# Complex weights' length by sine and cosine of the arc tangent, third-order norm roots, and all stores on one queue, in an S4 and shift-MLP kernel

## The chip, the cores and the metric

One core of a Trainium2 chip. Its engines run instruction streams of their own: TensorE (PE) multiplies matrices, VectorE (DVE) and ScalarE (ACT) work elementwise, GpSimd (POOL) is all but unused here, and SyncE (SP) issues most of the DMA transfers. ACT can issue transfers too. ACT evaluates functions from a table set, and an instruction of its own, ACT_TABLE_LOAD, changes the set. Waits between engines go over semaphores. The metric is the device time of the whole program in microseconds (us); lower is better.

## The reference

```python
x  = A_u                                   # 1 x 2048 x 512
xn = layernorm(x)

# s: 512 channels with 128 complex states each
dt = exp(log_dt)
K  = einsum("dn,dnl,dn->dl", C, exp(dt*A*l), dt*B).real     # 512 x 2048
s  = irfft(rfft(xn, 4096) * rfft(K, 4096))[:2048] + xn * Dskip

# g: token mixing by shifts, then an MLP
h  = gelu(layernorm(xn) @ w1)              # quarters of h shifted by +1, -1, +2, -2 rows
x1 = xn + shifted(h) @ w2
g  = silu(x1 + gelu(layernorm(x1) @ w3) @ w4)    # w3: 512 x 1376

out = x + s * g
```

The complex weights B·C·dt of the first part are kept as magnitude and phase. For a product with parts wr and wi the kernel forms the ratio `rat` of the smaller to the larger absolute value; the magnitude is the larger one times sqrt(1 + rat²), and the phase comes from the arc tangent of `rat`.

## The kernel before

The program is recorded first and issued afterwards. Functions such as `params`, `token_mixing`, `tables`, `mlp`, `products`, `gate`, `inverse` and `finish` record every operation in a `Plan`, through one recorder for each engine (`V` DVE, `A` ACT, `T` PE, `Q` SP) and one, `E`, for work that two may do. `Plan.order` then schedules the list. The table `DUE` gives the priority of every operation, the string `PIN` says which of two engines takes an `E` operation, and models of instruction fetch (`FETCH`) and of PE's clock say when an operation could start. Where PE would wait, the scheduler fills the wait with dummy matmuls of the identity matrix. So almost every instruction has line 499 in the profile, dummies have 498 and table loads 496; the tiles' names tell the work apart.

The work stands in this order. `loads` brings in the input X and the parameters. `params(0)` and `params(1)` form magnitude (`am`) and phase (`ph`) of the weights, half of the channels each, in tiles of 128x256: `tm` holds the temporaries `ta` and `tb`, `sr` holds `side` and `rat`, and `pn` holds the results. `token_mixing` takes norms (`ln_first`, `ln_second`, both through `rstd` with its tile `rs`), multiplies by w1 and w2 and starts the transform of xn. `tables` builds the exponentials and sines from which the convolution's kernel comes. `mlp` runs for eight groups of two of the 16 row blocks, `GROUPS` = 1 to 7 and then 0, between stages of the convolution. For each group w4's products are collected in two accumulators (tile `pa`), one for each row block, and DVE then adds them to X. `gate` applies Silu, `inverse` makes the convolution's result (`zin` in, `pc` out) and multiplies it in, and `finish` adds `xr`, which is u once more, and stores four strips of 32 partitions. The last group is handled in two pieces, one for each row block, all others in one: 36 stores in all.

`rstd` starts from a guess by integer arithmetic on the bits and makes three Newton steps of three DVE instructions each, in eleven calls. A store of `finish` is an `E` operation, so `PIN` gives it to SP's queue or to ACT's; 22 are on SP and 14 on ACT. The transfers of both queues take completion semaphores in turn from one set of eight (`DMAHW0` to `DMAHW7`), and each transfer waits until the one before it on its semaphore has ended.

Of the kernel before, what the change touches and what calls it, by code (L numbers as in the profile page):

```python
# [13 lines left out]
AF = mybir.ActivationFunctionType  # L14
# [5 lines left out]
P = 128  # L20
# [11 lines left out]
INV_2PI = float(np.float32(1.0 / (2.0 * np.pi)))  # L32
QUARTER_PI = float(np.float32(np.pi / 4.0))
# [63 lines left out]
class Op:  # L97
# [20 lines left out]
SPAN, LEFT, LEAST = 0.224, 0.3, 0.8  # L118
# [7 lines left out]
FETCH = 1.5, 5.0, 2.5, 0.5  # L126
# [168 lines left out]
class Plan:  # L295
# [115 lines left out]
    def order(self):  # L411
# [20 lines left out]
        while len(out) < len(ops):  # L432
# [22 lines left out]
            if e == "PE":  # L455
# [3 lines left out]
                if pick.fresh and t - free[e] > LEAST:  # L459
                    start = max(free[e], pick.free_at)  # L460
                    pick.fill = max(0, int((t - start - LEFT) / SPAN))
                    if pick.fill:
                        words.wait(start, pick.fill * SPAN, 4 * pick.fill, chan)
                        t = max(t, clock.run(start, pick.fill * SPAN))
# [1115 lines left out]
```

## Time and profile before

| | us |
| --- | --- |
| median of 3 runs | 536.68 |
| the runs | 536.22 to 537.21 |
| the profiled execution | 537.38 |
| its span | 535.6 |
| ACT's table loads, 48 of 1283 ns | 61.6 |
| first store issued (from the span's start) | 511.5 |
| last store issued | 532.9 |

The span runs from the first to the last instruction that the profiler saw; the execution's time has 1.8 us more around it. In a row, "128x256 f32<-128x256 f32" gives partitions by elements out and in, "x8" the number of records, and the bracket how long the engine stood idle before it and what ended that. A matmul of 32-bit numbers leaves two records. In the rows by group the figures behind the bar are busy time, mean nanoseconds of one, and idle time before. In the rows by tile the three figures are shortest, median and longest in nanoseconds, then the first and the last start. A row of windows gives the window, its length, and the busy time of PE, PE's weight loads, DVE, ACT and POOL; PEclk is the granted clock of PE as a share of full speed. A row of waits gives the total, the number and the longest. Times of rows are from the span's start.

### The profile page before, as it was taken

What the parts mean: (1) busy time and instruction counts of PE and PEld (TensorE: products, weight loads), DVE (VectorE), ACT (ScalarE), POOL (GpSimd) and SP (SyncE); (2) the same over time, 40 slices, a digit from 0 to 9 for tenths busy, and PEclk for the clock granted to TensorE, in tenths of its full rate; (3) what the DMA queues carried; (4) which work ended last, traced back from release to release, by engine and by line L of the source; (5) the groups of instructions that cost most, each with busy time, mean ns of one, the idle gap of its engine ahead of it and who ended that gap; (6) DMA issues with size and microseconds to landing.
All of it is one profiled execution on the core that took longest, in us unless ns stands there. A gap on an engine that the chain in (4) does not pass through costs nothing.

```text
span 535.6 us, 14336 instructions
## 1 busy us (share of the span) xinstructions
PE 511.1 (95%) x6055; PEld 333.1 (62%) x6055; DVE 450.9 (84%) x783; ACT 400.8 (75%) x597; POOL 0.7 (0%) x6
## 2 busy tenths in 40 slices
PE   8789999999999999999999999999999999999992
PEld 8776666774343666565676676666655666566650
DVE  6899999999999999999999999999553267754593
ACT  4999999999998999998989999885336315322420
POOL 0000000000000000000000000000000000000000
PEclk9899999999999999999999999999999999999997
DMA  7994689983886506456333643547989859979986
GB/s 192 258 222 160 227 249 254 281 233 121 296 269 221 101 7 163 140 194 178 112 129 70 180 158 107 118 164 207 251 332 320 282 175 286 258 234 275 310 252 186
DMA packets 95329, 109.44 MB, mean 204 GB/s; under 512 B 40289, under 2 KB 74337, under 8 KB 94369
## 3 DMA queue, kind: packets, MB, share of 16 engines
q1 hardware_dynamic: 94592, 106.95, 69.4%
q10 hardware_dynamic: 672, 1.57, 1.0%
q8 instruction: 47, 0.77, 0.6%
q14 instruction: 18, 0.14, 0.1%
HBM read 64.46 MB, written 37.75 MB: 191 GB/s over the span
## 4 chain that ended last, share of the span: by engine, by line
PE 68%; DVE 10%; ACT 10%; DMA 7%; issue 2%; SPq 2%; ACTq 0%; DVEq 0%
PE pb L499 22%; PE pa L499 22%; PE pd L499 13%; PE pc L499 11%; DVE pt L499 7%; DMA X<-in_A_u_dram 4%; ACT pt L499 3%; SPq L499 2%; ACT ue L499 2%; DVE X L499 1%; ACT L496 1%; DMA scr_Ud<-ue 1%; ACT wst L499 1%; DMA cst<-c_gp 1%; DMA rawC<-in_A_B_re_dram 1%
## 5 line engine op out<-in xcount | busy, mean ns | idle before, releaser
L499 PE MATMUL pb<-x1T,w3h 128*128 128x256 f16 (+1 forms) x1056 | 124.9, 273 | 0.0
L499 PE MATMUL pa<-w4h,ghl 128*128 128x512 f16 (+1 forms) x528 | 123.4, 380 | 0.0
L499 PEld LDWEIGHTS <-w3h 128*128 128x128 f16 (+1 forms) x1056 | 102.6, 100 | 28.8 <-issue 11.6
L499 PEld LDWEIGHTS <-ghl 128*128 128x128 f16 (+1 forms) x528 | 49.4, 98 | 60.6 <-issue 9.2
L499 ACT ACTIVATE g<-pb,wsc 128x512 f32<-128x512 f32 (+1 forms) x48 | 30.7, 650 | 47.6 <-PE pb L499 43.6
L499 ACT ACTIVATE pt<-pt 128x2048 f32<-128x2048 int32 x32 | 61.0, 1908 | 2.4 <-DVE pt L499 2.3
L496 ACT ACT_TABLE_LOAD x48 | 61.6, 1283 | 1.6 <-PEq L1568 0.7
L499 DVE TENSOR_TENSOR pt<-mag,pt 128x1024 f32<-128x1024 f32 x48 | 58.1, 1215 | 0.1
L499 PE MATMUL pd<-w,hT 128*128 128x512 f32 x116 | 53.3, 600 | 2.4 <-DVE X L499 1.9
L499 DVE SCALAR_TENSOR_TENSOR ghl<-g,wsc,ghl 128x512 f16<-128x512 f32 (+1 forms) x48 | 33.5, 700 | 11.6 <-ACT ghl L499 11.3
L499 ACT ACTIVATE mag<-par 128x128 f32<-128x128 f32 x160 | 41.1, 463 | 0.1
L499 ACT ACTIVATE ghl<-g,wsc 128x512 f16<-128x512 f32 (+1 forms) x35 | 24.0, 688 | 20.5 <-PE pa L499 19.0
L499 PEld LDWEIGHTS pd<-w,hT 128*128 128x128 f32 x116 | 21.1, 190 | 27.7 <-issue 23.3
L499 DVE TENSOR_TENSOR pt<-pt 128x2048 f32<-128x2048 f32 x16 | 36.4, 2281 | 0.9 <-ACT pt L499 0.9
L499 PEld LDWEIGHTS pc<-pt 128*32 128x32 f32 x2048 | 29.5, 110 | 8.4 <-issue 5.8
L499 PE MATMUL pc<-pt 128*32 128x64 f32 x2048 | 32.4, 220 | 1.9 <-DVE pt L499 1.0
L499 ACT ACTIVATE pt<-pt,halfpi 128x2048 f32<-128x2048 f32 x16 | 32.0, 1999 | 0.1
L499 PE MATMUL pb<-xT,w 128*128 128x256 f32 x128 | 29.6, 383 | 1.4 <-ACT xT L499 1.4
L499 DVE TENSOR_TENSOR pr<-pd,uin 128x1024 f32<-128x1024 f32 x16 | 19.3, 1219 | 11.5 <-PE pd L499 11.5
L499 PEld LDWEIGHTS pb<-xT,w 128*128 128x128 f32 x128 | 23.6, 190 | 7.8 <-ACT xT L499 3.3
L499 DVE TENSOR_TENSOR pr<-pd,kh 128x1024 f32<-128x1024 f32 x16 | 19.3, 1218 | 6.7 <-PE pd L499 6.0
L499 PE MATMUL pb<-xT,w1h 128*128 128x256 f16 x192 | 22.5, 273 | 0.0
(160 smaller groups left out, 787.8 us busy)
## 6 DMA issues: line engine op xcount, KB each, us to landing
wst<-in_B_w_dram SPq DMA_DIRECT2D x20, 512.0 KB, 5.1
scr_Ud<-ue SPq DMA_DIRECT2D x16, 512.0 KB, 3.9
uin<-scr_Ud SPq DMA_DIRECT2D x32, 256.0 KB, 4.3
cst<-c_gp SPq DMA_DIRECT2D x16, 384.0 KB, 4.0
scr_Uh<-uh SPq DMA_DIRECT2D x8, 512.0 KB, 3.2
scr_Kfa<-k1e SPq DMA_DIRECT2D x8, 512.0 KB, 3.7
kin<-scr_Kfa SPq DMA_DIRECT2D x16, 256.0 KB, 4.1
scr_Zda<-z1e SPq DMA_DIRECT2D x8, 512.0 KB, 5.0
```

Source lines behind the costliest of these rows:

```text
L496: self.engines["ACT"].preload_act_table_set(SETS[table])
L499: ins = [getattr(self.engines[op.eng], name)(*args, **kw).ins for name, args, kw in op.calls]
```

## The change

Six things change.

1. `rstd` makes one step of third order (four instructions) and one Newton step (three) in place of three Newton steps (nine).
2. `params` takes the length as max·(cos φ + rat·sin φ), with φ the arc tangent of `rat`. Arctan and two Sin run together from one table set; Square, Sqrt and the set of Sqrt go. DVE has two instructions more for each half.
3. All stores go to SP's queue.
4. For the last group, each pair of w4's products is two planned operations, one for each accumulator, where it was one.
5. Constants of the scheduler's models differ: `FETCH`, and a factor `FILLED` on the number of dummies in a wait. There are 34 dummies where there were 57, beside 36 at the start that stay.
6. `DUE` and `PIN` hold other values throughout, so that most instructions stand at other places. The rows further down show three places.

```diff
+CUBIC = 0.375 ** 0.5, -1.25 / 0.375 ** 0.5, 1.875
...
-FETCH = 1.5, 5.0, 2.5, 0.5
+FETCH = 1.8, 5.0, 2.8, 0.7
...
-                    pick.fill = max(0, int((t - start - LEFT) / SPAN))
+                    pick.fill = max(0, int((t - start - LEFT) * FILLED / SPAN))
...
     def rstd(dst, var, x, t, by=1.0):
         V.tensor_scalar(x, var, EPS, None, op0=ALU.add)
         guess(dst, x)
-        for f in (1.0, 1.0, by):
-            V.scalar_tensor_tensor(t, dst, -0.5 * f, dst, op0=ALU.mult, op1=ALU.mult)
-            V.tensor_mul(t, t, x)
-            V.scalar_tensor_tensor(dst, t, 1.5 * f, dst, op0=ALU.add, op1=ALU.mult)
+        V.scalar_tensor_tensor(t, dst, CUBIC[0], dst, op0=ALU.mult, op1=ALU.mult)
+        V.tensor_mul(t, t, x)
+        V.scalar_tensor_tensor(t, t, CUBIC[1], t, op0=ALU.add, op1=ALU.mult)
+        V.scalar_tensor_tensor(dst, t, CUBIC[2], dst, op0=ALU.add, op1=ALU.mult)
+        V.scalar_tensor_tensor(t, dst, -0.5 * by, dst, op0=ALU.mult, op1=ALU.mult)
+        V.tensor_mul(t, t, x)
+        V.scalar_tensor_tensor(dst, t, 1.5 * by, dst, op0=ALU.add, op1=ALU.mult)
...
-        A.activation(ta, rat, AF.Square)
-        A.activation(tb, ta, AF.Sqrt, bias=1.0)
-        V.tensor_mul(am, am, tb)
+        with plan.together(table=TABLES[AF.Arctan]):
+            A.activation(ph, rat, AF.Arctan)
+            A.activation(ta, ph, AF.Sin)
+            A.activation(tb, ph, AF.Sin, bias=halfpi[:, 0:1], scale=-1.0)
+        V.tensor_mul(ta, ta, rat)
+        V.tensor_add(ta, ta, tb)
+        V.tensor_mul(am, am, ta)
         by_step(am, am, ld)
-        A.activation(ph, rat, AF.Arctan)
...
-            for r in range(4):
-                E.store(ov[ORDER[r]][:, x], X[32 * r : 32 * r + 32, x])
+            by_r(X[:, x, c], ov[:, :, :, x][..., c], True)
...
-                with plan.together(cost=DOWN):
-                    for i in range(2):
+                for some in ((0,), (1,)) if g == GROUPS[-1] else ((0, 1),):
+                    with plan.together(cost=DOWN * len(some) / 2):
+                        for i in some:
```

The first place is ACT in the first half of `params`. Before (`tm<-sr` is Square, `pn<-sr` the Arctan, the `tm<-tm` between the loads Sqrt; `EB` and `mag` are exponentials):

```order
L499 ACTIVATE tm<-sr 128x256 [waits DVE_49]
L496 ACT_TABLE_LOAD
L499 ACTIVATE pn<-sr 128x256
L496 ACT_TABLE_LOAD
L499 ACTIVATE tm<-tm 128x256 [waits Activation_49]
L499 ACTIVATE wst,ssq<-wst 128x1024 [waits DMAHW4_49]
L496 ACT_TABLE_LOAD
L499 ACTIVATE EB<-par 128x128 x12
```

The same place in the changed program, from the load before the Arctan on (`tm<-pn` and `tm<-pn,halfpi` are the sines):

```order
L496 ACT_TABLE_LOAD
L499 ACTIVATE pn<-sr 128x256 [waits DVE_49]
L499 ACTIVATE tm<-pn 128x256 [waits Activation_49]
L499 ACTIVATE tm<-pn,halfpi 128x256
L496 ACT_TABLE_LOAD
L499 ACTIVATE mag<-par 128x128 x8
L499 ACTIVATE EB<-par 128x128 x12
L499 ACTIVATE pn<-pn,ld 128x128 [waits DVE_49]
```

Three loads have become two, and the load of the weights' squares (`wst`) has moved behind the exponentials.

The second place is the end of PE's stream: the last w4 products (`pa`), of which `ghl_486` and `ghl_488` are the left sides and each has three for either accumulator, and the last inverse transforms (`pc`). Before:

```order
L499 LDWEIGHTS ghl_488 [waits DVE_49]
L499 MATMUL pa_97<-w4h_205,ghl_488 128x512
L499 LDWEIGHTS ghl_488
L499 MATMUL pa_97<-w4h_205,ghl_488 128x512
L499 MATMUL pc_98<-zin_556,is2_82 32x256 [waits DMAHW7_49,DVE_49]
L499 MATMUL pc_98<-zin_556,is2_82 32x256 x7
L499 MATMUL pc_98<-zin_557,is2_82 32x256 [waits DMAHW5_49]
L499 MATMUL pc_98<-zin_557,is2_82 32x256 x7
```

The end of PE's stream in the changed program:

```order
L499 LDWEIGHTS ghl_486
L499 MATMUL pa_97<-w4h_201,ghl_486 128x512
L499 LDWEIGHTS ghl_488
L499 MATMUL pa_97<-w4h_205,ghl_488 128x512 [waits DVE_49]
L499 LDWEIGHTS ghl_488
L499 MATMUL pa_97<-w4h_205,ghl_488 128x512
L499 LDWEIGHTS ghl_488
L499 MATMUL pa_97<-w4h_205,ghl_488 128x512
L499 MATMUL pc_98<-zin_557,is2_82 32x256 [waits DMAHW2_49]
L499 MATMUL pc_98<-zin_557,is2_82 32x256 x7
```

The products of the second accumulator now stand by themselves at the end, the last three with a wait for DVE, and the first set of inverse transforms (`zin_556`) stands ahead of this place.

The third place is the end of ACT's stream, with its stores and the last Silu (`X<-X` 128x512). Before:

```order
L499 DMA out_dram<-X 32x1024 [waits DMAHW2_49,DVE_49]
L499 DMA out_dram<-X 32x1024 [waits DMAHW4_49]
L499 ACTIVATE X<-X 128x512 [waits DVE_49] x2
L499 DMA out_dram<-X 32x1024 [waits DMAHW6_49]
L499 DMA out_dram<-X 32x512 [waits DMAHW0_49,DVE_49,Activation_49]
L499 DMA out_dram<-X 32x1024 [waits DMAHW2_49]
L499 DMA out_dram<-X 32x512 [waits DMAHW4_49,DVE_49,Activation_49]
L499 DMA out_dram<-X 32x512 [waits DMAHW5_49]
L499 DMA out_dram<-X 32x512 [waits DMAHW7_49]
```

In the changed program SP's stream ends with all of the last group's stores, and ACT's with the Silu:

```order
L499 DMA out_dram<-X 32x512 [waits DMAHW1_49,DVE_49,Activation_49]
L499 DMA out_dram<-X 32x512 [waits DMAHW2_49]
L499 DMA out_dram<-X 32x512 [waits DMAHW3_49]
L499 DMA out_dram<-X 32x512 [waits DMAHW4_49,DVE_49,Activation_49]
L499 DMA out_dram<-X 32x512 [waits DMAHW5_49]
L499 DMA out_dram<-X 32x512 [waits DMAHW6_49]
```

The 14 stores of ACT stand on SP, and their completion semaphores now follow one another in SP's own order.

More of the change, by code (lines that the diff above doesn't have):

```diff
@@ L117 @@
 WINDOW, LOW, HIGH, HALF = 3.4133, 0.64, 0.87, 0.6
-SPAN, LEFT, LEAST = 0.224, 0.3, 0.8
+SPAN, LEFT, LEAST, FILLED = 0.224, 0.3, 0.8, 0.87
 SCRATCH = 512
@@ L647 @@
     E = Either(plan)
-    xv = u[0].rearrange("(t r s) d -> r t s d", r=4, s=S)
-    ov = out[0].rearrange("(t r s) d -> r t s d", r=4, s=S)
+    xv = u[0].rearrange("(t b a s) d -> a b t s d", a=2, b=2, s=S)
+    ov = out[0].rearrange("(t b a s) d -> a b t s d", a=2, b=2, s=S)
     dram = ctx.enter_context(tc.tile_pool(name="dram", bufs=1, space=DRAM))
@@ L832, in loads @@
     def loads():
-        by_r(X[:, 0:2], xv[:, :, 0:2])
+        by_r(X[:, 0:2], xv[:, :, :, 0:2])
         load_w(w1, w1s, stile)
@@ L1192, in gate @@
     def gate(g):
-        for x, _ in pieces(g):
-            A.activation(X[:, x], X[:, x], AF.Silu)
+        for x, _, c in pieces(g):
+            A.activation(X[:, x, c], X[:, x, c], AF.Silu)
     def inverse(hf, g):
@@ L1209, in inverse @@
                 return
-            for x, k in pieces(g):
-                V.tensor_mul(X[:, x], X[:, x], pair[:, k])
+            for x, k, c in pieces(g):
+                V.tensor_mul(X[:, x, c], X[:, x, c], pair[:, k, c])
             return
@@ L1221, in finish @@
             xr[q] = at(xrs.pop(), [P, 4, D], F32, "xr")
-            by_r(xr[q], xv[:, :, 4 * q : 4 * q + 4])
-        for x, k in pieces(g):
-            V.tensor_add(X[:, x], X[:, x], xr[q][:, 2 * (g % 2) : 2 * (g % 2) + 2][:, k])
-            for r in range(4):
-                E.store(ov[ORDER[r]][:, x], X[32 * r : 32 * r + 32, x])
+            by_r(xr[q], xv[:, :, :, 4 * q : 4 * q + 4])
+        for x, k, c in pieces(g):
+            V.tensor_add(X[:, x, c], X[:, x, c], xr[q][:, 2 * (g % 2) : 2 * (g % 2) + 2][:, k, c])
+            by_r(X[:, x, c], ov[:, :, :, x][..., c], True)
     def pow2_scale(cols, dst_s, dst_inv, target):
@@ L1443, in pieces @@
         if g != GROUPS[-1]:
-            return [(slice(2 * g, 2 * g + 2), slice(0, 2))]
-        return [(2 * g + k, k) for k in range(2)]
+            return [(slice(2 * g, 2 * g + 2), slice(0, 2), slice(0, D))]
+        return [(2 * g + k, k, slice(0, D)) for k in range(2)]
     def mlp(g):
@@ L1476, in mlp @@
                 fn = FT[j][1]
-                with plan.together(cost=DOWN):
-                    for i in range(2):
-                        for lg, lw in ((0, 0), (0, 1), (1, 0)):
-                            T.matmul(
-                                accs[i], ghl[:fn, lg, a, i * P : (i + 1) * P], w4t[jp][:fn, a, lw],
-                                start=j == 0 and lg == 0 and lw == 0,
-                                stop=j == len(FT) - 1 and lg == 1,
-                            )
+                for some in ((0,), (1,)) if g == GROUPS[-1] else ((0, 1),):
+                    with plan.together(cost=DOWN * len(some) / 2):
+                        for i in some:
+                            for lg, lw in ((0, 0), (0, 1), (1, 0)):
+                                T.matmul(
+                                    accs[i], ghl[:fn, lg, a, i * P : (i + 1) * P], w4t[jp][:fn, a, lw],
+                                    start=j == 0 and lg == 0 and lw == 0,
+                                    stop=j == len(FT) - 1 and lg == 1,
+                                )
         if g == GROUPS[-1]:
             A.activation(warm[:fr], g32[:fr, 0, 0:1], AF.Silu)
-        for x, k in pieces(g):
-            V.scalar_tensor_tensor(X[:, x], duo[0][:, k], a4, X[:, x], op0=ALU.mult, op1=ALU.add)
+        for x, k, c in pieces(g):
+            V.scalar_tensor_tensor(X[:, x, c], duo[0][:, k, c], a4, X[:, x, c], op0=ALU.mult, op1=ALU.add)
     def token_mixing():
```

38 lines of the change are left out of this document (19 added, 19 removed), and 181 rows, old and new, of the table DUE.

## The prediction

> **What bounds the kernel now.** First the page: its shares of busy time, and the chain that ended last. Then the busy time of each engine in the two stretches into which the program falls, 32 to 176 us and 176 to 526 us from the span's start.
>
> ```profile
> span 535.6 us, 14336 instructions
> PE 511.1 (95%) x6055; PEld 333.1 (62%) x6055; DVE 450.9 (84%) x783; ACT 400.8 (75%) x597; POOL 0.7 (0%) x6
> PE 68%; DVE 10%; ACT 10%; DMA 7%; issue 2%; SPq 2%; ACTq 0%; DVEq 0%
> core 0: us, PE busy (x) PEld busy (x) DVE busy (x) ACT busy (x) POOL busy (x), PEclk, DMA share, GB/s
> 32.00:176.00 144.00, 137.23 (x1557) 86.89 (x1557) 142.28 (x290) 140.85 (x199) 0.00 (x0) 1.00 0.79 228
> 176.00:526.00 350.00, 347.67 (x4310) 221.22 (x4310) 280.54 (x399) 234.86 (x327) 0.00 (x0) 1.00 0.66 194
> ```
>
> From 176 to 526 us PE is busy for 347.67 of 350 us, with DVE and ACT far below: whatever is saved on those two there is worth nothing. From 32 to 176 us all three engines are full (PE lacks 6.8 us, DVE 1.7, ACT 3.2), so work taken from ACT or DVE counts there, though only in part, because the other one and PE stand right behind. Before 32 us PE has little of its own to do, and after 526 us nothing but the end of the output is left. So the change can pay in three places: the start, the full stretch, and the tail.
>
> **ACT: the length of the weights.** The first half, before:
>
> ```profile
> 14.59 0.42 ACT L499 ACTIVATE tm<-sr 128x256 f32<-128x256 f32 x1
> 15.02 1.28 ACT L496 ACT_TABLE_LOAD   x1
> 16.32 0.42 ACT L499 ACTIVATE pn<-sr 128x256 f32<-128x256 f32 x1
> 16.75 1.28 ACT L496 ACT_TABLE_LOAD   x1
> 18.04 0.42 ACT L499 ACTIVATE tm<-tm 128x256 f32<-128x256 f32 x1
> 19.52 1.28 ACT L496 ACT_TABLE_LOAD   x1
> L499 ACT ACTIVATE pt<-pt,halfpi 128x2048 f32<-128x2048 f32 x16 | 32.0, 1999 | 0.1
> L499 ACT ACTIVATE pt<-pt 128x2048 f32<-128x2048 int32 x32 | 61.0, 1908 | 2.4 <-DVE pt L499 2.3
> ```
>
> These are Square, a load, Arctan, a load, Sqrt, and the load for the exponentials. The change takes away Square, Sqrt and the load before Sqrt: 0.42 + 0.42 + 1.28 = 2.12 us a half. It adds two sines of the same shape. No sine of 128x256 is in the trace. The nearest row is the Arctan's 0.42, and a bias from a tile lengthens the large sines from 1908 to 1999 ns, so I take 0.42 + 0.51 = 0.93. The bounds are 0.7, if each overlaps the next by about 0.1, and 1.2, if the sine itself cost 0.1 more. Per half ACT is thus relieved by 1.2 us (0.9 to 1.4), 2.4 in both. The new order also runs the 128x128 exponentials of the tables behind others of their set once more often ahead of 176 us, which spares one more load of 1.28; two loads come in later, where ACT has 115 us to spare. Together 3.7 us less on ACT up to 176 us.
>
> The Trainium skill, page "ScalarE: Activation LUTs", section "What ACT_TABLE_LOAD costs", gives a switch of sets about 1283 ns and a drain of about 1380 ns behind it, 2.66 us together. The trace has the next activation 1.30 us after a load's start (15.02 to 16.32) and so shows no drain; by the page the three loads would be worth 8 us and not 3.9.
>
> **DVE: roots and weights.**
>
> ```profile
> L499 DVE SCALAR_TENSOR_TENSOR rs<-rs x66: 128/154/170, 20.6 to 382.9; 128x4 f32<-128x4 f32 x24, 128x2 f32<-128x2 f32 x24, 128x8 f32<-128x8 f32 x18
> L499 DVE TENSOR_TENSOR rs<-rs x33: 143/154/168, 21.4 to 379.9; 128x4 f32<-128x4 f32 x12, 128x2 f32<-128x2 f32 x12, 128x8 f32<-128x8 f32 x9
> 32.33 0.15 DVE L499 SCALAR_TENSOR_TENSOR rs<-rs 128x4 f32<-128x4 f32 x1
> 32.40 0.28 DVE L499 TENSOR_SCALAR tr<-tr 128x256 f32<-128x256 f32 x1
> 5.51 0.43 DVE L499 TENSOR_TENSOR tm<-tm 128x256 f32<-128x256 f32 x1
> 5.85 0.16 DVE L499 TENSOR_SCALAR ld<-ld 128x4 f32<-128x4 f32 x1
> ```
>
> The 99 root instructions (66 and 33) are eleven calls of nine; at seven each, 77 are left, 22 fewer. One takes 0.154 us, but the next starts 0.07 after it (32.33 to 32.40), so the 22 are worth 1.5 to 3.4 us; I take 1.8, near the first, since DVE is full and its rows overlap. The weights gain a mul and an add in each half: four of 0.43 us, or 0.34 from start to start (5.51 to 5.85), so 1.4 us. Net 0.4 us less on DVE (from 2.0 less to 0.2 more).
>
> **What of this reaches the end.** ACT and DVE have 3.7 + 0.4 = 4.1 us less to do in a stretch where each waits for the other in turn; if both share it, each finishes 2.05 us sooner. PE must follow: there it stands for 6.8 us and runs dummy matmuls besides. I give it two thirds of the 2.05, **1.4 us**. The bounds are 0 (the new order loses as much in waits) and 3.7 (all of ACT's saving counts). What hides the rest is PE's own 137 us.
>
> The start of the real work isn't expected to move:
>
> ```profile
> 30.99 1.09 ACT L499 COPY xT<-pd 128x1024 f32<-128x1024 f32 x1
> 20.12:23.53 3.41, 1.57 (x12) 1.37 (x13) 3.38 (x20) 3.40 (x13) 0.00 (x0) 1.00 1.00 217
> 23.53:26.94 3.41, 3.41 (x18) 3.41 (x17) 3.41 (x13) 3.41 (x16) 0.00 (x0) 0.50 1.09 291
> 22.64 7.15 PE L498 MATMUL pd<-ident 128*128 128x128 f32 x48
> 29.63 1.04 PE L499 MATMUL pd<-ident,x 128*128 128x128 f32 x8
> 32.13 1.99 PE L499 MATMUL pb<-xT,w 128*128 128x256 f32 x8 [1.25 <-ACT xT L499]
> 79.24 1.60 PE L498 MATMUL pd<-ident 128*128 128x128 f32 x12
> ```
>
> The first product waits for ACT's copy of the transposes, and these for DVE's norm and the load of X, not for the weights. The dummies (x48 records are 24 instructions) fall from 57 to 34; they fill waits, so fewer of them save nothing where PE waits anyway.
>
> **The tail.**
>
> ```profile
> 517.46 6.65 PE L499 MATMUL pa<-w4h,ghl 128*128 128x512 f16 x30
> 524.04 1.09 PE L499 MATMUL pc<-zin,is 64*32 64x256 f32 x32
> 524.15 1.41 DVE L499 SCALAR_TENSOR_TENSOR X<-pa,wsc,X 128x512 f32<-128x512 f32 x2 [1.09 <-PE pa L499]
> 524.94 1.29 ACT L499 ACTIVATE X<-X 128x512 f32<-128x512 f32 x2 [3.89 <-DVE X L499]
> 525.60 0.69 DVE L499 TENSOR_TENSOR X<-X,pc 128x512 f32<-128x512 f32 x1
> 527.65 0.69 DVE L499 TENSOR_TENSOR X<-X,xr 128x512 f32<-128x512 f32 x1
> 511.49 21.83 SPq L499 DMA_DIRECT2D out_dram<-X  x22
> L499 SPq DMA_DIRECT2D out_dram<-X x22: 314/366/733, 511.5 to 532.9; - x22
> L499 ACTq DMA_DIRECT2D out_dram<-X x14: 321/387/591, 511.5 to 529.4; - x14
> SPq L499 <- DMA out_dram<-X: 9.9, 5, 5.4
> 532.43 0.88 SPq L499 DMA_DIRECT2D out_dram<-X  x2
> 516.83 4.79 SPq L499 DMA_DIRECT2D out_dram<-X  x8
> DMA to landing us min/median/max: 1.6/2.2/5.6
> ```
>
> PE's last accumulation ends at 517.46 + 6.65 = 524.11, the last add at 528.34, but the last store is issued at 532.90: SP stood 9.9 us in five waits for stores, the longest 5.4. Each store waits for the one eight before it on its completion lane, both queues share the eight lanes, and ACT issues its stores in order behind a Silu that waits 3.89 us for DVE. That hold goes when SP issues all stores.
>
> Against that stands the split: in the new order PE runs the first accumulator's three matmuls to the end, the inverse transform of one half ahead of it (0.55 of the 1.09 us), and the second accumulator's last three matmuls after DVE has read the first. They take 30 records in 6.65, so 0.65 us for three. The first accumulator is thus done at 524.11 + 0.55 - 0.65, 0.1 earlier. Then DVE reads it for 0.7, PE needs 0.65 and 0.55 more, DVE reads the second, and the two multiplies and adds follow at 0.69 each: the first add ends 3.8 us after the first accumulator, the second 5.15, or 5.05 after 524.11 where it was 4.23. **The split costs 0.8 us** (0 to 0.8, nothing if the wait is not real).
>
> SP then has seven more stores to issue after the first add's own; at 0.46 us (the last two of before take 0.88, and start 0.47 apart) the last is issued 3.8 + 3.2 = 7.0 us after the first accumulator, 6.9 after 524.11, where it was 8.8: **1.9 us gained**, of which the queue gives 2.7 and the split takes 0.8. At the pace with stalls (4.79 for eight, 0.60) it is 0.9; at the bare issue time of 0.37 it is 2.5. From the last issue to the end I leave 2.7 us, 532.90 to 535.6.
>
> Sum: 1.4 + 1.9 = 3.3 us. The span goes from 535.6 to 532.3, the profiled execution, which has 1.8 us around the span, from 537.38 to 534.1. That execution lies 0.7 above the median; I take the 3.3 off the median: **533.4 us**.
>
> **Rivals.**
>
> *A larger gain.* All of ACT's 3.7 us comes through and the tail as above: 5.6 us, 531.1. For it speaks that ACT lacks only 3.2 us there; against it that DVE, fuller, loses but 0.4.
>
> *One queue is too slow.* 36 stores stand on SP in a row, from 510.1 (511.49 less 1.4) on. If a step is over 0.56 us, the queue and not the last add decides: (529.6 - 510.1) / 35. At 0.60 the last issue comes at 531.1, 534.9 us in all; at 0.65, where landings last 5.2 us on eight lanes, at 532.9, and the time is 536.6, no change; from 0.69 it would be slower. For it speak the 0.60 of the eight and the longest landing, 5.6; against it the median landing of 2.2, which lets eight lanes take a store in 0.28. The Trainium skill, page "DMA: Bandwidth & Descriptors", section "Issuing engines are not separate DMA queues", says that several issuing engines save only the time a sequencer needs to issue. By that rule the change loses on the queue: 14 issues of 0.39 us go to SP, 5.4 us, and no hold ends. The 5.4 us for which SP stood show what the rule leaves out.
>
> *The clock: slower than before.* After a stretch with PE busy 1.57 of 3.41 us the clock was 0.50 for the next, and cost nothing, since 22.64 to 29.79 held dummies. In the new order 21 dummies stand ahead of the first product, not 48: 27 fewer at 0.27 us (x12 records, so six, in 1.60 at 79.24), 7 us less PE work just before 32 us. If that leaves two such stretches of real work at half the clock, each loses 1.7 us, 3.4 together; if the middle gain is lost with it, -1.9 + 3.4 gives 538.2. One stretch alone, with the middle gain kept, still ends faster, at 535.1. It decides from the second on. Against it: PE waits for ACT and DVE in these stretches, so some of the loss is covered.
>
> **How the numbers follow.** Forecast 0.58, larger gain 0.12, one queue too slow 0.15, clock 0.15. About 0.2% (1.07 us) is what a measurement of this kernel tells from no change: faster is below 535.6, slower above 537.75. Faster takes the forecast but 0.02, all of the larger gain and 0.04 of the slow queue: 0.72. The same takes 0.02 of the forecast, 0.09 of the queue and 0.03 of the clock: 0.14. Slower has 0.12 of the clock and 0.02 of the queue: 0.14. The forecast's own range is 531.7 (2.5 in the middle, 2.5 in the tail) to 535.8 (0 and 0.9). To hold 8 in 10 the range goes from 531.0, with most of the larger gain, to 537.0, with most of the slow queue; what is left out is the clock's case and the far ends.
>
> **What would show it.** ACT's rows for each half: Arctan and two sines with no load between them, and 47 loads in all. The end of PE's work in the stretch to 176 us, some 1.4 us sooner. In the tail: no issue on ACT, no wait of SP for a store over 2 us, PE's last three matmuls of the accumulation behind DVE's read, the last issue near 529.6, the end 2.7 us after. Wrong it would be if the granted clock falls below 1.00 between 32 and 60 us, if PE stands longer than 6.8 us up to 176 us, or if SP's steps are 0.6 us and more.

## The result: slower, and the profile after

| | before | after |
| --- | --- | --- |
| median of 5 runs each, us | 536.22 | 541.22 |
| the runs, us | 534.94 to 537.21 | 538.85 to 543.66 |
| the profiled execution, us | 537.38 | 540.27 |
| its span, us | 535.6 | 538.5 |
| last accumulation of w4 done, first accumulator, us from the span's start | 524.11 | 527.09 |

The ratio is 1.0081, with an interval of 1.006 to 1.0102: the changed kernel is slower by some 4.3 us, where 3.3 us less were forecast. The profiled execution is one of the quicker of its five; its span is 2.9 us longer. That whole difference is there when the last accumulation ends (3.0 us), so the forecast missed in both of its terms: in this execution nothing was gained before the tail, and nothing in it. (Three executions of the experiments below, of 550 to 1023 us at a granted clock of 0.94 or less, are left out.)

From the page after (span; busy time, share and instructions of each engine; shares in the chain that ended last):

```profile
span 538.5 us, 14209 instructions
PE 506.6 (94%) x6009; PEld 327.2 (61%) x6009; DVE 456.3 (85%) x765; ACT 394.9 (73%) x596; POOL 0.7 (0%) x6
PE 62%; ACT 22%; DVE 7%; DMA 4%; issue 3%; SPq 2%; ACTq 0%
```

The windows after (length, then busy time of PE, PE's loads, DVE, ACT and POOL, granted clock, DMA share, GB/s):

```profile
32.00:176.00 144.00, 136.06 (x1509) 86.73 (x1511) 139.56 (x271) 139.39 (x199) 0.00 (x0) 1.00 0.78 225
176.00:526.00 350.00, 347.32 (x4357) 220.26 (x4346) 285.98 (x400) 229.06 (x322) 0.00 (x0) 1.00 0.67 192
```

From 32 to 176 us every engine stands longer than before: PE 7.9 us (6.8), DVE 4.4 (1.7), ACT 4.6 (3.2). ACT has less to do, but has moved up in the chain that ended last, from 10% to 22%.

ACT and DVE in the first half of `params`, after:

```profile
15.75 0.42 ACT L499 ACTIVATE pn<-sr 128x256 f32<-128x256 f32 x1
16.20 0.42 ACT L499 ACTIVATE tm<-pn 128x256 f32<-128x256 f32 x1
16.52 0.49 ACT L499 ACTIVATE tm<-pn,halfpi 128x256 f32<-128x256 f32 x1
17.03 1.28 ACT L496 ACT_TABLE_LOAD   x1
17.05 0.43 DVE L499 SCALAR_TENSOR_TENSOR pn<-pn,sr 128x256 f32<-128x256 f32 x1 [1.24 <-ACT tm L499]
```

Arctan and the two sines run with no load between them, and the sines take 0.42 and 0.49 us, as forecast. The last row holds something that was not: DVE's first instruction on the phase is let go by ACT's `tm`, the sines, and not by the Arctan.

PE around 96 us, after (time, duration, instruction, and in the bracket the idle time and what ended it; "issue" is nothing that the profile can name):

```profile
93.02 1.99 PE L499 MATMUL pc<-pt 128*32 128x64 f32 x128
94.95 1.27 PE L499 MATMUL pb<-xT,w1h 128*128 128x256 f16 x10
98.54 1.69 PE L499 MATMUL pb<-xT,w1h 128*128 128x256 f16 x14 [2.33 <-issue]
101.00 1.47 PE L499 MATMUL pb<-xT,w1h 128*128 128x256 f16 x12 [0.78 <-ACT hT L499]
```

In the middle of one product, with its operands there, PE stops for 2.33 us. Before, PE's waits of this kind came to 0.9 us, in two; the longer is a stop of the same sort, as the section on the stop shows:

```profile
176.38 0.31 PE L499 MATMUL pc<-pt 128*32 128x64 f32 x6 [0.70 <-issue]
```

To see where time is lost, the two traces can be laid side by side at the same work: the time at which PE has done so many us of real matmuls (dummies left out, each weighted with the granted clock), worked out from all PE rows. Less than nothing is earlier than before.

```text
before stands at   30.1   71.6   76.4   83.5   93.5   99.7   120.5   135.9   157.0   178.6   238.8   519.8
after             -1.01  -1.96  -1.86  -0.26  -0.28  +2.66   +2.32   +2.76   +2.91   +1.63   +2.85   +2.92
a_shift18         -1.27  -2.27  -2.38  -0.33  -0.43  +0.21   +0.72   +2.17   +2.43   +1.16   +2.77   +1.81
```

The changed kernel is 1.0 us ahead at 30.1 us (its first product starts at 31.64 in place of 32.13), is 2 us ahead at 72 to 76 us, loses that lead by 83 us (PE stands there until ACT has copied `ue`, in both kernels, and that copy starts at 79.55 in place of 80.42), and drops 2.9 us at once at the stop. (The second row is an experiment, below. Its last entry is rough: by the start of the same product, in the last accumulation, a_shift18 is 0.3 us ahead of the changed kernel and not 1.1.)

The tail, after, from the timeline: PE's last accumulations, DVE's first read and two of its adds, and SP's stores.

```profile
524.32 2.77 PE L499 MATMUL pa<-w4h,ghl 128*128 128x512 f16 x12
527.92 0.81 PE L499 MATMUL pa<-w4h,ghl 96*128 96x512 f16 x3 [0.84 <-DVE X L499]
527.12 0.75 DVE L499 SCALAR_TENSOR_TENSOR X<-pa,wsc,X 128x512 f32<-128x512 f32 x1 [0.43 <-PE pa L499]
530.22 0.69 DVE L499 TENSOR_TENSOR X<-X,xr 128x512 f32<-128x512 f32 x1
531.55 0.69 DVE L499 TENSOR_TENSOR X<-X,xr 128x512 f32<-128x512 f32 x1
512.99 23.20 SPq L499 DMA_DIRECT2D out_dram<-X  x36
```

The stores by tile (shortest, median and longest issue in ns; first and last start):

```profile
L499 SPq DMA_DIRECT2D out_dram<-X x36: 314/421/1397, 513.0 to 535.8; - x36
```

The adds come where the forecast put them: 3.8 and 5.15 us after the first accumulator (530.91 and 532.24 less 527.09). The last store does not: it is issued at 535.77, 8.7 us after the accumulator and 3.5 us after the last add, in place of 7.0. Other executions with the same tail (all below) differ: from the accumulator to the span's end it is 11.4 us here and 11.5 before, but 11.6 in a_fewer15, 10.9 in a_again and a_war, and 10.2 in a_shift18 and a_dummies18. Single issues of SP take 0.6 to 1.7 us in them where most take 0.42; why is not known.

### The profile page after: what moved, and what is told of

Same layout as the page of the kernel before. It is cut to its first block, busy times and chain, and to the rows that moved or that the text cites. A ratio compares the mean times of both kernels' runs of the same rounds, so it can differ in the third digit from the quotient of the medians.

```text
span 538.5 us, 14209 instructions
## 1 busy us (share of the span) xinstructions
PE 506.6 (94%) x6009; PEld 327.2 (61%) x6009; DVE 456.3 (85%) x765; ACT 394.9 (73%) x596; POOL 0.7 (0%) x6
## 4 chain that ended last, share of the span: by engine, by line
PE 62%; ACT 22%; DVE 7%; DMA 4%; issue 3%; SPq 2%; ACTq 0%
PE pb L499 21%; PE pa L499 20%; PE pd L499 12%; PE pc L499 9%; ACT pt L499 6%; ACT mag L499 4%; DVE pt L499 3%; ACT L496 3%; DMA X<-in_A_u_dram 2%; SPq L499 2%; DMA cst<-c_gp 2%; DVE X L499 2%; ACT ue L499 1%; ACT wst L499 1%; ACT hT L499 1%
## 5 line engine op out<-in xcount | busy, mean ns | idle before, releaser
L499 DVE TENSOR_TENSOR pt<-mag,pt 128x1024 f32<-128x1024 f32 x48 | 57.9, 1217 | 0.0
L499 ACT ACTIVATE ghl<-g,wsc 128x512 f16<-128x512 f32 (+1 forms) x31 | 21.0, 682 | 22.1 <-PE pa L499 12.8
L499 PEld LDWEIGHTS <-w1h 128*128 128x128 f16 x192 | 18.5, 98 | 8.1 <-issue 5.9
```

The lines of the kernel that those rows point to most:

```text
L499: ins = [getattr(self.engines[op.eng], name)(*args, **kw).ins for name, args, kw in op.calls]
```

## The experiments

In each kernel the order, the engines and the dummies are written out as the kernel before or the changed one has them, so that the scheduler can move nothing else, and only the edit shown differs (a_war and a_all also shift a few rows of `params` by one place). Names with b_ start from the kernel before, those with a_ from the changed one. Ratios are against runs of the kernel before on the same chip; 0.002 is about 1.1 us.

### One part at a time, in the old order

**b_onequeue**: the 14 stores of ACT go to SP, nothing else.

```diff
 PIN (for the 14 stores that ACT issued)
-0
+1
```

> The kernel before, its order word for word, with the 14 stores of ACT given to SP. The forecast's term: SP's 5.4 us hold goes and the end comes 2.7 us sooner, about 533.5. Its rival (one queue too slow): 36 stores at about 0.47 us behind the first one at 511.5 would let the last one start at 528 or as soon as the last add allows; if the queue decides instead, the gain is under 1 us, about 535.5 to 536.5.

Ratio 0.9974 (0.9962 to 0.9986), 1.4 us faster, half of the 2.7 that the forecast gave the queue. It is the one kernel here that beats both. Its stores by tile, and how long they took to land:

```profile
L429 SPq DMA_DIRECT2D out_dram<-X x36: 314/420/517, 510.9 to 530.9; - x36
DMA to landing us min/median/max: 1.7/2.2/4.7
```

Its last add, from the timeline:

```profile
527.04 0.69 DVE L429 TENSOR_TENSOR X<-X,xr 128x512 f32<-128x512 f32 x1
```

The longest landing is 4.7 us where it was 5.6, but 36 issues from 510.9 to 530.9 are 0.57 us a step on average, just over the 0.56 that the rival "one queue is too slow" gave as its point; from 520.24 on they run without a gap, 24 in 10.6 us, at 0.46 a step, and the last goes out 3.1 us after the last add. So SP's queue decides the end, at the step that the forecast took, because it was behind before the last adds came.

**b_newmath**: the new roots and sines in the old order (the diff is that of the change). **b_newmath2**: the same, with the phase's first step into another tile.

```diff
-        V.scalar_tensor_tensor(ph, ph, QUARTER_PI, side, op0=ALU.subtract, op1=ALU.mult)
-        V.scalar_tensor_tensor(ph, ph, QUARTER_PI, wr, op0=ALU.subtract, op1=ALU.mult)
+        V.scalar_tensor_tensor(side, ph, QUARTER_PI, side, op0=ALU.subtract, op1=ALU.mult)
+        V.scalar_tensor_tensor(ph, side, QUARTER_PI, wr, op0=ALU.subtract, op1=ALU.mult)
```

> The kernel before, its order word for word, with the new roots (22 DVE instructions fewer) and the new length of the weights (Arctan and two sines together, two table loads fewer, four DVE instructions more), and nothing else of the change. The forecast's middle term without the third spared load: 0.7 to 1.0 us faster, about 535.4. Theory O: the same. Theory F: the same, since PE's instructions are as before; only the times at which they run shift a little. A rival: nothing, 536.2, since the order was laid out for the old costs.

> The kernel before, its order word for word, with the new roots and the new length as in the run that took 2.6 us more, but the phase's first DVE instruction writes to another tile and waits for the Arctan alone. Theory W: DVE's wait at 15.5 to 17.9 us shrinks by about 1 us in each half, and 1 to 2 us of the 2.6 come back, 537 to 538. If the sines' place in ACT's order or the four added DVE instructions are the loss: no change, 539.

Ratios 1.0048 (1.0033 to 1.0062) and 1.0011 (0.9998 to 1.0023): 2.6 us slower, of which 2.0 come back. DVE's first step on the phase, before:

```profile
16.76 0.42 DVE L499 SCALAR_TENSOR_TENSOR pn<-pn,sr 128x256 f32<-128x256 f32 x1 [1.77 <-ACT pn L499]
```

The same step, and PE's first product, in b_newmath:

```profile
17.90 0.42 DVE L429 SCALAR_TENSOR_TENSOR pn<-pn,sr 128x256 f32<-128x256 f32 x1 [2.42 <-ACT tm L429]
33.82 1.99 PE L429 MATMUL pb<-xT,w 128*128 128x256 f32 x8 [0.88 <-ACT xT L429]
```

And in b_newmath2:

```profile
16.67 0.43 DVE L429 SCALAR_TENSOR_TENSOR sr<-pn,sr 128x256 f32<-128x256 f32 x1 [1.57 <-ACT pn L429]
32.70 1.99 PE L429 MATMUL pb<-xT,w 128*128 128x256 f32 x8 [0.88 <-ACT xT L429]
```

The step overwrites `ph`, and the sines, unlike Square and Sqrt, read `ph`: an instruction that only writes over its operand has to wait for all its readers. That holds DVE for 1.1 us in the first half, and the first product, 32.13 before, comes at 33.82. With the wait gone it comes at 32.70, and the new arithmetic is about even in an order that was made for the old one, though PE stands for 1.28 us at 177.93 us in it, where the kernel before has 0.70.

### The stop of PE

The trace shows PE's instructions arriving: the instruction queue's 47 transfers carry 0.77 MB, 16.4 KB each. The Trainium skill, page "Advanced Engine Details and Errata", section "ISA Cache", has lines of 16 KB, 256 instructions; the trace agrees: 47 blocks of 256 make 12032 instructions, and the changed kernel's PE has 12018 records of products and loads. Counting PE's instructions (loads of weights too) beside these transfers, block k is asked for about when PE has run 256·k + 150 instructions (no row shows the request; the earliest transfers begin 0.6 us behind that point), and the first that PE cannot run without it is number 256·k + 449 (there it stood), so 299 instructions have to last as long as the transfer needs to come. Worked out so for the block that PE stood for, and the same one before:

```text
                    asked    moved             instruction 256k+449 runs
before, k = 3       86.82    89.59 to 90.55     95.17   no stop
after, k = 3        91.53    96.27 to 97.20     98.54   2.33 us idle ahead of it
```

In the changed kernel the 256 instructions of `pc<-pt` (128 products, 128 loads, 1.99 us) fall between the two, and the transfer was 4.7 us in coming; the instruction ran 1.34 us after the block had landed. Which instructions fall between depends on how many stand ahead, so on the number of dummies. Four kernels move the boundary:

```diff
 b_dummies8    (8 more dummies, 32 instructions, in the first wait)
-FILLS = {96: 24, 174: 24, 472: 6, 660: 3}
+FILLS = {96: 32, 174: 24, 472: 6, 660: 3}
 a_dummies18   (18 more at the start)
-FILLS = {94: 2, 98: 3, 139: 5, 170: 5, 172: 6, 462: 13}
+FILLS = {94: 20, 98: 3, 139: 5, 170: 5, 172: 6, 462: 13}
 a_fewer15     (15 fewer)
+FILLS = {94: 2, 139: 1, 170: 1, 172: 2, 462: 13}
 a_shift18     (18 more, into a bank that nothing waits for)
+EXTRA = {98: 18}
...
+            for _ in range(EXTRA.get(op.idx, 0)):
+                pad = next(v for k, v in self.spare.items() if "pb0" in k[0])
+                self.engines["PE"].matmul(pad, *self.filler, start=True, stop=True)
```

> The kernel before, its order word for word, with 8 more dummy matmuls in PE's first long wait, which has 2.0 us idle left for them; they add 32 instructions ahead of all others and no work that anything waits for. Theory F: the places at which PE needs its next block of instructions move by 32 instructions into the dense runs of small products; two blocks that had 6 us from their request to their need get 2.4 and 2.7, and the kernel is 1.5 to 4 us slower (538 to 540), with PE idle for nothing else at two or three places. Theory O: no change, 536.2.

> The changed kernel's order word for word with 18 more dummies (72 instructions) in PE's first long wait, which has 8.7 us of idle time for their 4.2. Theory F: the block needed at instruction 1217 is now asked for over 6 us ahead, so the stop near 96 us goes or shrinks to under 1 us; instead the blocks 11, 24 and 31 get 2.7, 3.1 and 4.4 us, and stops of 1 to 3 us come at about 158 and 290 us; in all 0 to 2 us slower than the changed kernel. Theory O: nothing moves, 541.2, and the stop stays where it was.

> The changed kernel's order word for word without 15 of the 21 dummies ahead of the first product (60 instructions fewer). Theory F: the block at instruction 1217 gets 6.7 us, so the stop near 96 us goes; one block (28, near 330 us) gets 2.9 us; 1 to 2.5 us faster than the changed kernel, 539 to 540. The clock's rival: with still less work on PE before 32 us the granted clock falls to 0.5 in a stretch of real work, and it is 1.5 to 3 us slower. Theory O: no change.

> The changed kernel's order word for word, with the 18 dummies more of the run before, now behind the transposes of the first wait and into another tile, where nothing waits for them (there they held PE's start up by 2 us). Theory F: the block needed at instruction 1217 is asked for in time, the stop of 2.1 to 2.3 us near 96 us and the 0.8 behind it go, nothing else moves: 2 to 3 us faster than the changed kernel, 537.5 to 538.8. Theory O (what is lost lies in waits of the new order): the stop goes, but PE waits for DVE or ACT right behind it instead; 540 to 541.

b_dummies8 is slower by 1.5 us (1.0028, 1.0016 to 1.004), with the same work and 8 dummies more, but not by its stop, as its trace shows below. a_fewer15 stays where the changed kernel is (1.0092, 1.0071 to 1.0113); its stop at 96 us is gone and another stands one block later. PE's rows:

```profile
99.95 1.99 PE L430 MATMUL pc<-pt 128*32 128x64 f32 x128
101.88 0.50 PE L430 MATMUL pb<-xT,w1h 128*128 128x256 f16 x3
104.29 5.43 PE L430 MATMUL pb<-xT,w1h 128*128 128x256 f16 x33 [1.91 <-issue]
```

The windows of the stop and of what follows it:

```profile
101.70:105.10 3.40, 1.49 (x31) 1.09 (x20) 3.30 (x5) 3.39 (x3) 0.00 (x0) 0.99 1.01 196
105.10:108.50 3.40, 3.40 (x19) 2.44 (x17) 3.40 (x5) 3.37 (x4) 0.00 (x0) 0.51 0.48 119
```

In the second the clock is at half, of which more below. In b_dummies8 the stop is a smaller one, at the block that the count names (k = 8):

```profile
126.29 1.98 PE L429 MATMUL pc<-pt 128*32 128x64 f32 x125
129.01 0.30 PE L429 MATMUL pc<-pt 128*32 128x64 f32 x3 [0.74 <-issue]
```

That places the stop where the count says, but doesn't explain the 1.5 us: the 0.70 us at 176.38 of before are gone, the products behind that place start level (176.49 and 176.62 us), and the 1.3 us by which the last accumulation is late (525.39 in place of 524.11) come further on, in small steps.

a_dummies18 (1.0082, 1.0067 to 1.0096) has no stop at 96 us either, and those of 1 to 3 us that were expected at 158 and 290 us didn't come; but its dummies held up the transposes of the start, and the first product came at 33.29, 1.65 us later, most of what the stop had cost. a_shift18 puts them where nothing waits: 1.0045 (1.0028 to 1.0063), some 1.9 us faster than the changed kernel. So between the medians the stop is worth about 1.9 us.

The profiled executions show where the stop's time goes. In the table +2.66 at 99.7 us becomes +0.21 without the stop, but at 238.8 us the two kernels are level again, +2.85 with the stop and +2.77 without. The last products into the first accumulator, in a_shift18:

```profile
524.01 2.77 PE L434 MATMUL pa<-w4h,ghl 128*128 128x512 f16 x12
```

They start 0.3 us ahead of the changed kernel's (524.32); those of a_dummies18 start at 524.23. a_shift18 loses its lead at a wait with a half clock behind it at 121 us (next section) and at a stop of its own, 0.44 us at 157.27. So by the end of PE's work in these executions little is left of the stop's time, and 1.2 of the 1.5 us between the two spans lie in SP's issues behind it. That the stop alone costs the 1.9 us is not shown.

**a_again** is the changed kernel once more.

> The changed kernel itself once more, for a second profile. Theory F (PE runs dry of instructions): a stop of PE on nothing, next to the move of a 16-KB block of its stream, is there again, near 96 us as in the first profile or at another of the places where the block is needed under 5.5 us after it was asked for (there are seven); 540 to 542. Theory O (waits of the new order): PE's waits on DVE and ACT repeat within 0.3 us, and the stop near 96 us may be gone without the time getting better than 539.

1.0085 (1.0067 to 1.0103), with the stop at the same instruction (2.11 us): it comes again.

### The rest of the new order

Of the 4.3 us, 2.4 are left in a_shift18. Three kernels look into the tail and the phase's wait: **a_swap** runs the second accumulator's last three products ahead of DVE's read, as before (two places in the order exchanged), **a_war** has the other tile of b_newmath2, **a_all** both and the 18 dummies.

```diff
 DUE
-    ... 1789, 1796, 1774, 1794, 1801, ...
+    ... 1789, 1794, 1774, 1796, 1801, ...
```

> The changed kernel's order word for word, but PE's last three products of the second accumulator stand ahead of DVE's read of the first one, so that PE doesn't wait for it. Theory O (the loss lies in waits of the new order, the split among them): PE's wait of 0.84 us before the last three products goes, and the whole is 0.5 to 0.9 us faster than the changed kernel (541.2), about 540.5. Theory F (PE runs dry of instructions because a 16-KB block of its stream comes late): no more than that either, and the 2.3 us idle on nothing near 96 us stays in the trace.

> The changed kernel's order but for one row a half, with the phase's first DVE instruction writing to another tile, so that it no longer overwrites what the two sines read. Theory W (that instruction, in order on DVE, waits for both sines): DVE's idle time of 1.24 us before it shrinks to about 0.4 and up to 0.8 us is gained, 539.6 to 540.4. If DVE is not what sets the start in this order: no change.

> The changed kernel with three edits: the 18 dummies placed as above, the phase's first DVE instruction to another tile, and PE's last three products of the second accumulator ahead of DVE's read of the first. Theory F with W and the split: 2 to 3, 0 to 0.8 and 0.3 to 0.9 us add up, 536 to 538, so the changed kernel's loss against the one before (536.0 to 536.5) is gone but for about 1 us. Theory O: 539.5 to 541.

a_swap 1.006 (1.0042 to 1.0077), a_war 1.0093 (1.0069 to 1.0118), a_all 1.0043 (1.0026 to 1.006). The wait on the phase shows no cost in the new order. What the split costs is not settled: a_swap is 1.1 us below the changed kernel with intervals that overlap, and a_all no better than a_shift18. Then the old arithmetic and the old queues, in the new order:

```diff
 a_oldmath and a_s18_oldmath (the old roots, Square and Sqrt; roots not shown)
-        with plan.together(table=TABLES[AF.Arctan]):
-            A.activation(ph, rat, AF.Arctan)
-            A.activation(ta, ph, AF.Sin)
-            A.activation(tb, ph, AF.Sin, bias=halfpi[:, 0:1], scale=-1.0)
-        V.tensor_mul(ta, ta, rat)
-        V.tensor_add(ta, ta, tb)
-        V.tensor_mul(am, am, ta)
+        A.activation(ta, rat, AF.Square)
+        A.activation(tb, ta, AF.Sqrt, bias=1.0)
+        V.tensor_mul(am, am, tb)
...
+        A.activation(ph, rat, AF.Arctan)
 a_s18_twoq (14 stores on ACT again)
-            by_r(X[:, x, c], ov[:, :, :, x][..., c], True)
+            for r in range(4):
+                E.store(ov[r // 2, r % 2][:, x][..., c], X[32 * r : 32 * r + 32, x, c])
```

> The changed kernel's order word for word with the old roots (nine DVE instructions a call) and the old length of the weights (Square and Sqrt, two table loads more). By the forecast's middle term it is 0.7 to 1.5 us slower than the changed kernel, 542 to 543. If the phase's first DVE instruction, which overwrites what the sines read and so waits for them, costs as much as the spared loads bring, no change: 541; if it costs more, faster than the changed kernel, 539 to 540.

> a_shift18 with Square and Sqrt and the old norm roots put back, and the order kept: 49 table loads in place of 47. By the forecast's middle term (1.4 us) and one more load at the start it is 1.4 to 2.6 us slower than a_shift18: 540 to 541.1 us, ratio 1.007 to 1.0095. By the trace of a_oldmath, which lay 2.4 us behind the changed kernel before its stop near 100 us, 2.4 us slower, near 1.009. Rival: what a_oldmath lost (4.2 us against the changed kernel) was the arithmetic alone and not a worse stop: 4 us slower, near 1.012.

> The changed kernel with the 18 dummies of a_shift18 (538.55 us, ratio 1.0045) and, of the last two groups' stores, the 14 that ScalarE issued before back on ScalarE at their old places. By the forecast's term for one queue it is 2.7 us slower than a_shift18, 541.2 us and a ratio near 1.0095; by what b_onequeue measured alone, 1.4 us slower (near 1.007). Rival: in the new order the last adds come late and in clumps and SyncE issues its 36 stores without a gap until 3.5 us after the last add, so that one queue gives nothing here: within 0.5 us of a_shift18, 1.0035 to 1.0055, or below.

a_oldmath is 1.0157 (1.0142 to 1.0171), but it has a stop of 2.38 us and a half clock behind it; without that stop, a_s18_oldmath is 1.0052 (1.0036 to 1.0068) and a_s18_twoq 1.005 (1.0034 to 1.0067), against the 1.0045 of a_shift18. In the new order the new arithmetic is thus worth 0.4 us and the one queue 0.3, neither told from nothing. What is left, some 2.4 + 0.4 + 0.3 = 3.1 us, falls to the new order, with the split, the other dummies and a stop of 0.44 us in it. That is an estimate: no kernel here has the new order with all the old parts.

The trace of a_shift18 points at one place, between +0.72 at 120.5 us and +2.17 at 135.9. PE's rows there:

```profile
118.54 0.38 PE L434 MATMUL pd<-m,ones 1*128 1x1 f32 x2
120.56 5.40 PE L434 MATMUL pd<-w,hT 128*128 128x512 f32 x8 [1.65 <-DVE wsc L434]
```

The windows of that wait and of what follows it:

```profile
117.70:121.10 3.40, 1.75 (x70) 1.34 (x60) 3.33 (x8) 3.39 (x11) 0.00 (x0) 1.00 0.86 241
121.10:124.50 3.40, 3.40 (x6) 1.33 (x5) 3.40 (x4) 3.40 (x14) 0.00 (x0) 0.52 0.52 186
```

The same place before:

```profile
118.96 0.38 PE L499 MATMUL pd<-m,ones 1*128 1x1 f32 x2
119.27 1.48 PE L499 MATMUL pb<-xT,w1h 128*128 128x256 f16 x12
121.23 3.70 PE L499 MATMUL pd<-w,hT 128*128 128x512 f32 x8 [0.48 <-DVE wsc L499]
```

Before, twelve products stood between the sum over the partitions and the product that needs its scale; in the new order they have been run already, and PE stands for 1.65 us. It was busy for 1.75 of 3.40 us, and for the next 3.40 the clock is 0.52: eight products take 5.40 us in place of 3.70. (The changed kernel has the same wait, 1.28 us at 122.16, but not the half clock.) **a_s18_wsc** moves the scale ahead of a 2.27-us square on DVE; **a_s18_wsc2** also moves a sum of another channel ahead, so that DVE needn't idle.

```diff
 DVE (a_s18_wsc)
-TENSOR_TENSOR pt<-pt 128x2x1024
 TENSOR_SCALAR wsc<-pd 128x1
+TENSOR_TENSOR pt<-pt 128x2x1024
```

> a_shift18 (538.55 us, ratio 1.0045) with one pair of VectorE's instructions exchanged: the product's scale, wsc<-pd at 120.37 us, ahead of the 2.27-us square pt<-pt before it, so that TensorE's pd<-w,hT need not wait 1.65 us for it at 120.56. If that uncovered wait, and the stretch at half the clock behind it (8 matmuls in 5.40 us in place of 3.70), are what the new order loses there, the first product starts 1.0 to 1.3 us earlier with the clock at 1.00 behind it, and the time falls by 1.0 to 3.0 us, to 535.5 to 537.5 (ratio 0.999 to 1.003). Rival: VectorE, busy without a gap there, is late with the next thing instead (it idles some 0.85 us for the sum), and less than 0.7 us is left: 1.0035 or more.

> As a_s18_wsc, but a 1.22-us sum (pt<-pab) of another channel also moved ahead of the scale, so that VectorE needn't idle for it: the scale comes 0.9 us earlier than in a_shift18 and not 1.3, and VectorE loses nothing. If the uncovered wait is the loss, 0.9 us and whatever the clock loses behind it come back (ratio 0.999 to 1.003); if VectorE's idle time ate the gain of a_s18_wsc, this one is faster than that; rival: no gain, 1.0035 or more.

1.0032 (1.0018 to 1.0045) and 1.0039 (1.0024 to 1.0054): 0.7 and 0.3 us less than a_shift18, not told from nothing. PE and DVE in a_s18_wsc:

```profile
119.65 3.70 PE L434 MATMUL pd<-w,hT 128*128 128x512 f32 x8 [0.25 <-DVE wsc L434]
125.37 0.99 PE L434 MATMUL pc<-pt 128*32 128x64 f32 x56 [1.78 <-DVE pt L434]
137.76 7.13 PE L434 MATMUL pd<-w,hT 128*128 128x512 f32 x16 [1.02 <-DVE X L434]
119.43 0.16 DVE L434 TENSOR_SCALAR wsc<-pd 128x1 f32<-128x1 f32 x1 [0.72 <-PE pd L434]
```

The product starts 0.9 us earlier at full clock, and PE then waits 1.78 us for DVE's `pt` and 1.02 for its `X`. The wait has only moved: here DVE is the bound, and a wait taken from PE at one place comes back at the next. In which of these waits the order's 3.1 us lie stays open; no single one of those tried holds them.

## Why the prediction was wrong

**ACT's saving** was right in each part: no load between Arctan and the sines, the sines at 0.42 and 0.49, 47 loads in the page. **DVE's** missed a wait, the phase's step behind the sines: 2.0 us in the old order, none to be seen in the new one.

**"What of this reaches the end"** is the step that failed: two thirds of 2.05 us, 1.4, were to come through, with PE's own 137 us as the cover and 0 as the worst. The lower bound was wrong. It let the new order lose what the arithmetic gains, and no more; the new order lost some 5.0 us, the 4.3 and the 0.4 and 0.3 that arithmetic and queue bring in it. Of these, 1.9 go when the dummies are moved so that PE's stop is gone, and 3.1 are left, in waits that stay open. The trace of before could show how full the engines are, but not what a new order of 1800 operations makes of it: PE's lead of 2 us at 72 to 76 us was real, and was gone at the next wait.

**"Fewer of them save nothing"**, of the dummies, was right as to their time and wrong as to their number: they are instructions, and decide where the blocks end. That PE can run out of instructions was in the kernel's own scheduler (`FETCH`), and in the profile as rows "<-issue"; it had no term in the sum. The kernel before has such a stop itself, the 0.70 us at 176.38.

**The start** was expected not to move and came 0.5 us sooner (31.64), which made no difference.

**The tail**, 1.9 us forecast, gave 0.1: from the first accumulator to the span's end 11.4 us in place of 11.5; in other executions of the same tail it lay between 0.1 lost and 1.3 gained. The split was right (the adds at 3.8 and 5.15), and so was the step of 0.46, as the usual one (0.47 here); on average it is 0.53 from 521.39 on, with issues of 1.40 and 0.83 us among them. Wrong was "SP then has seven more stores to issue after the first add's own": ten were still to go out after that add, since the adds of the groups ahead came late and in a clump, and SP ran without a gap from 521.39. The forecast had eight there. Two more steps at 0.47, 0.2 us until the issue under way was done, and 0.4 for one issue of 0.83 make 1.6 us of the 1.7 by which the last issue was late. The queue's 2.7 was mis-sized even alone, at 1.4.

**The rivals.** "One queue is too slow" was right in its mechanism, SP and not the last add decides, and at its point, 0.57 in b_onequeue; its own sum then has the last issue at 511.5 + 35 · 0.57 = 531.5 us in place of 532.9, the 1.4 us that b_onequeue measured. "The clock" ended on the right side for another reason: the granted clock is 1.00 from 32 to 176 us of the profiled execution, and the start held.

But the clock's mechanism is in the runs, behind the waits of PE at 100 to 125 us: 0.51 and 0.52 in a_fewer15 and a_shift18. It may be part of what the stop costs. A window of 3.4 us at half the clock takes 0.003 off an execution's mean clock. Of the changed kernel, a_again and a_war, which have the stop, eight executions have a mean of 0.983 to 0.985 and took 538.85 to 541.00 us; nine have 0.977 to 0.982 and took 540.93 to 543.66. The six of a_shift18 have 0.985 to 0.990 and took 538.17 to 539.64. In a_oldmath the stop falls into one window, 98.18 to 101.59 us with PE busy 1.03 us, and the next is at half; in the changed kernel's trace it falls across two, and none is. No trace of one of the nine is there to show the same.

Of the signs, one that said "wrong" was there, PE standing longer than 6.8 us up to 176 us. The order decided it, and the forecast had treated the order as a carrier of the savings and not as a change of its own.

## What to carry to other kernels

Where a change re-plans the whole order, price the order apart from the edits: freeze it, and run each edit in the old order and the old edits in the new one; here the edit that pays, one queue, was worth 1.4 us in the old order and next to nothing in the new. Ask of each operand that is overwritten who now reads it. And count PE's instructions as a resource: dense small matmuls behind a block's request can stop PE with its data ready. But judge a stop by what is left of it at the end: here 2.3 us were down to 0.3 when PE's work ended.

## What the hardware showed that was not expected

Stops of PE with no wait to name came at instructions 256·k + 449: 1217 in the changed kernel, a_again, a_war and a_oldmath (2.11 to 2.38 us), 1473 in a_fewer15 (1.91), 2497 in b_dummies8 (0.74), and at k = 12 in the kernel before (0.70) and b_newmath2 (1.28); two smaller ones fit too, 0.53 us in a_fewer15 and 0.44 in a_shift18. PE went on 1.2 to 1.5 us after the 16.4-KB block had landed. One of 1.28 us in a_fewer15, at 261.45 us, doesn't fit the count. From the request, by the count above, to the transfer a block of the changed kernel took 0.6 to 7.2 us, the program's first one aside; what holds it up for so long was not found.

Behind a window with PE busy 1.75 of 3.40 us (51%), and one with 1.49 (44%), the clock was at half for the next one; neither was idle. The Trainium skill, page "TensorE: Matmul & The Clock Gate", section "What's actually happening", has the clock fall after a window that is idle; by these rows a window half idle can do it. It doesn't always. In a_s18_wsc, a window with PE busy for 1.63 us and the next:

```profile
122.28:125.69 3.41, 1.63 (x33) 0.67 (x35) 3.41 (x4) 3.16 (x11) 0.00 (x0) 1.00 0.34 124
125.69:129.10 3.41, 3.41 (x147) 2.42 (x137) 3.41 (x5) 3.41 (x11) 0.00 (x0) 1.00 0.51 175
```

The changed kernel's window from 94.48 to 97.89, with 1.73 us, left the clock at 1.00 too. So PE's busy share alone doesn't decide near one half, and what does was not found.
